# Gating a Pool load queue on VectorE, with a new order of all steps: attention and an ELU layer on one Trainium2 core

## The chip, the cores and the metric

The kernel runs on one NeuronCore of a Trainium2 chip (trn2). The metric is the device time of one execution in microseconds (us); less is better. The engines work side by side, each through its own instructions in program order: TensorE (PE for its matmuls, PEld for its weight loads), VectorE (DVE), ScalarE (ACT), GpSimd (POOL) and SyncE (SP). Here POOL does little but issue loads and SP little but issue stores and transposing copies.

## The reference, cut to what matters

Attention with 16 extra keys ("beacons") ahead of 576 tokens, for 8 batches and 8 heads of width 64; then two matrix products with an ELU between them on all 4,608 tokens.

```python
scores = scale * np.matmul(q, k_all.transpose(0, 1, 3, 2))   # k_all: 16 beacon keys, then k
scores = np.where(causal, -1000000000.0, scores)
a = np.exp(scores - scores.max(-1, keepdims=True))
a /= a.sum(-1, keepdims=True) + 1e-09
attn_out = np.matmul(a, v_all)
# ... (cut: heads side by side, x is 4608 x 512)
h = x @ w_in                                                  # 512 x 2048
g = np.where(h > 0.0, h, np.exp(np.minimum(h, 0.0)) - 1.0)
out = g @ w_out                                               # 2048 x 512
```

All inputs and the output are float32. The kernel computes in 16 bits and accumulates in float32.

## The kernel before

The kernel is a list of 1,597 short words, each of which is one step. A loop reads the list from the front and emits the step's instructions. The framework orders engines by data: it adds the semaphores that the tiles' reads and writes require. So the list sets only the order of instructions on each engine, which step takes which buffer, and with that when an engine may start.

```python
    for word in """
    warm.11.128.bank.0 lq.0.0.0.2 lq.0.1.0.2 lq.0.1.4.8 lq.0.0.2.4 lq.0.1.2.4 id tri lq.0.0.4.8 bs
    # ... (cut: 1,597 words in all)
    s.9.3 os.8.3
    """.split():
        f, *args = word.split(".")
        op[f](*[int(a_) if a_.isdigit() else a_ for a_ in args])
```

The first number of a word is the batch b (or the token tile t: tiles 0 and 1 have 256 tokens, 2 to 9 have 512), and then come head pair p, chunk or block. What each kind of word does, and where:

| word | engine | step |
|---|---|---|
| lq, ld, lv, lb, wi, wo | POOL issues | loads that cast float32 to 16 bits: q and k of batches 0 and 1 (lq) into SBUF; q and k of later batches (ld, four parts each) into DRAM; v (lv, five parts) and beacon v (lb); w_in (wi, eight parts) and w_out (wo, four) |
| ct | SP issues | two transposing copies of q and k of one head pair, DRAM to SBUF |
| s, os | SP issues | store of an output tile |
| T, S, L/W, Y/Z | PE | transposes (batches 0 and 1), scores, sums and value products of batch 0, of later batches |
| F, G | PE | product with w_in; product with w_out, in four quarters |
| warm | PE | filler matmuls on zeros |
| x, n/N, e | ACT | exponential of scores; reciprocal of the sums as exp(-ln); exponential of the ELU |
| m, a, M/V, r, g | DVE | causal mask; partial sums; scaling by the reciprocal; min(e,1)-1; max(h, r) |
| cp, o | ACT (A) or DVE (V) | copies out of PSUM |
| cb | DVE | beacon keys into the key tile |

The loads, all on GpSimd's queue, and the transposing copies on SyncE's:

```python
    @step
    def lq(b, i, h0, h1):

        if (b, i) not in st:
            st[b, i] = attn.tile([PR, H, R, D], BF16, tag=f"et{next(slots['et'])}", bufs=1, name="stg")
        nc.gpsimd.dma_start(
            out=st[b, i][:, h0:h1, :, :].rearrange("p h r d -> p h (r d)"),
            in_=(q, k)[i][b, h0:h1, :, :].rearrange("h (p r) d -> p h (r d)", r=R),
        )
    # ... (cut)
    @step
    def ld(b, i, s0):

        if (b, i) not in st:
            st[b, i] = dram.tile([S, H, D], BF16, tag=f"qk{i}", name="qkd")
        s1 = s0 + S // 4
        nc.gpsimd.dma_start(
            out=st[b, i][s0:s1], in_=(q, k)[i][b, :, s0:s1].rearrange("h s d -> s h d"))

    # ... (cut)
    @step
    def lv(b, j):
        r0 = NB if j == 0 else 0
        n_ = kc[j] - r0
        nc.gpsimd.dma_start(
            out=v_tile(b)[r0:r0 + n_, j, :, :],
            in_=v[b, :, ilo[j]:ilo[j] + n_, :].rearrange("h s d -> s h d"))

    # ... (cut)
    def wi(part_, g_):

        f0, f1 = DF // 4 * part_, DF // 4 * (part_ + 1)
        nc.gpsimd.dma_start(out=w_in16[:, 2 * g_:2 * g_ + 2, f0:f1], in_=wi_v[:, g_, :, f0:f1])
    # ... (cut)
    @step
    def wo(i):
        nc.gpsimd.dma_start(out=w_out16[:, 4 * i:4 * (i + 1), :], in_=wo_v[:, 4 * i:4 * (i + 1), :])
```

```python
    @step
    def cb(b, p):
        nc.vector.tensor_copy(out=keys(b, p)[:, 1, 0:NB], in_=bkT[:, p, NB * b:NB * (b + 1)])

    @step
    def ct(b, p):

        for i in range(2):
            nc.sync.dma_start_transpose(
                out=keys(b, p)[:, i, NB:SK], in_=st[b, i][:, 2 * p:2 * p + 2, :].rearrange("s h d -> s (h d)"))

```

The scores of one chunk and the value products (with ones in place of v: the sums), as TensorE has them:

```python
    def score(b, p, s, c0, c1, o0):

        t = keys(b, p)
        for (j, qa, qe, col) in lays[b]:
            a, e = max(c0, col), min(c1, col + qe - qa)
            if a >= e:
                continue
            for h in range(2):
                nc.tensor.matmul(
                    out=s[:, h, o0 + a - c0:o0 + e - c0],
                    lhsT=t[D * h:D * (h + 1), 1, P * j:P * (j + 1)],
                    rhs=t[D * h:D * (h + 1), 0, NB + qa + a - col:NB + qa + e - col],
                    start=True, stop=True, skip_group_check=True,
                )

    # ... (cut)
    def quad(b, g, qa, qe, t, half, first):


        v16 = vt[b]
        pcs = [(j, max(a, qa), min(e, qe), c + max(a, qa) - a) for (j, a, e, c) in lays[b]
               if max(a, qa) < min(e, qe)]
        for n, (j, a, e, c) in enumerate(pcs):
            for i in range(4):
                h, p = 4 * g + i, 2 * g + i // 2
                nc.tensor.matmul(
                    out=t[32 * i:32 * (i + 1), a - qa:e - qa],
                    lhsT=ones[0:kc[j], :] if half is None else v16[0:kc[j], j, h, half::2],
                    rhs=ets[b, p][0:kc[j], i % 2, c:c + e - a],
                    start=(first and n == 0), stop=(n == len(pcs) - 1), skip_group_check=True)
```

The exponential of the scores, the logarithm and exponential that make the reciprocal (batch 0's step n.0.A), and the chain of the second half, where each F takes a PSUM bank until its g has read it:

```python
    @step
    def x(b, *k_):
        s, (p, c0, c1, o0) = et_part(b, *k_)
        if (b, p) not in ets:
            ets[b, p] = attn.tile([P, 2, ECOLS], FP16, tag=f"et{next(slots['et'])}", bufs=1, name="et")
        nc.scalar.activation(
            out=ets[b, p][:, :, c0:c1], in_=s[:, :, o0:o0 + c1 - c0],
            func=AFT.Exp, bias=0.0, scale=SCALE)

    # ... (cut)
    @step
    def n(b, g):
        src = lt[b, g]
        w = src.free_size()
        rl = rls[b, g] = attn.tile([P, 640], FP32, tag="rl", name="rl")
        dst = rl[:, 0:w]
        nc.scalar.activation(
            out=dst.rearrange("p (g c) -> p g c", g=2) if len(src.shape) == 3 else dst,
            in_=src, func=AFT.Ln, bias=0.0, scale=1.0)
        nc.scalar.activation(out=dst, in_=dst, func=AFT.Exp, bias=0.0, scale=-1.0)
    # ... (cut)
    @step
    def F(t, i):

        a, e = tiles[t]
        w = e - a
        h = hp[t, i] = bank(name="hps").rearrange("c (n w) -> c n w", w=w)
        k_ = a // TT
        for n_ in range(512 // w):
            fc = i * (512 // w) + n_
            for cc in range(NCC):
                nc.tensor.matmul(
                    out=h[:, n_, :], lhsT=w_in16[:, cc, P * fc:P * (fc + 1)],
                    rhs=xt[k_][:, cc, a - TT * k_:e - TT * k_], start=(cc == 0), stop=(cc == NCC - 1))
    # ... (cut)
    @step
    def e(t, i):
        eb[t, i] = melt.tile([P, 512], FP32, tag="e", name="e")
        nc.scalar.activation(out=eb[t, i], in_=flat(hp[t, i]), func=AFT.Exp, bias=0.0, scale=1.0)

    @step
    def r(t, i):
        rb[t, i] = melt.tile([P, 512], FP16, tag="r", name="r")
        nc.vector.tensor_scalar(
            out=rb[t, i], in0=eb[t, i], scalar1=1.0, scalar2=1.0, op0=ALU.min, op1=ALU.subtract)

    @step
    def g(t, i):
        w = tiles[t][1] - tiles[t][0]
        gt = gpool.tile([P, 512 // w, w], FP16, tag="g", name="gt")
        nc.vector.tensor_tensor(out=flat(gt), in0=flat(hp[t, i]), in1=rb[t, i], op=ALU.max)
    # ... (cut)
    @step
    def G(t, tb_, qd):
        if qd == 0:
            ob[t, tb_] = bank(name="ops")
        for fc in range(4 * qd, 4 * qd + 4):
            nc.tensor.matmul(
                out=ob[t, tb_], lhsT=gts[t, fc][:, P * tb_:P * (tb_ + 1)], rhs=w_out16[:, fc, :],
                start=(fc == 0), stop=(fc == NFC - 1))
    # ... (cut)
    @step
    def o(t, tb_, e_):
        osb = melt.tile([P, DM], FP32, tag="osb", bufs=5, name="osb")
        ENGINE[e_](out=osb, in_=ob[t, tb_])
        ob[t, tb_] = osb

    @step
    def s(t, tb_):
        row = tiles[t][0] + tb_ * P
        nc.sync.dma_start(out=out[row:row + P, :], in_=ob[t, tb_])
```

Which slot of a pool of buffers a step takes is read from digit strings, one for each pool ("et" for exponentials, "bank" for the four single PSUM banks, "qk" for the eight key tiles, "S" for the two double banks).

Of the kernel before, what the change touches and what calls it, by code (L numbers as in the profile page):

```python
# [17 lines left out]
def kernel(  # L18
# [11 lines left out]
    nc = tc.nc  # L30
    P = 128

    B, H, S, D = q.shape
# [23 lines left out]
            "085476123807654128370564128370564281"),  # L57
        "bank": (
            "03210320123012302100120312031230120201310312031203123211031023102312021032032123"
            "01231031021230210310321032101230201231023023021301201321032023012301231021001231"  # L60
            "231230123012302302310201302302310310"),
        "qk": (
            "07654132067541230657412630752413"),
        "S": (
            "01010101010101010101010101010101101010101010100110001101010101010010100101101011"
            "010101010100110101010010100101001011010101100101010101100101"),
# [512 lines left out]

    for word in """  # L580
    warm.11.128.bank.0 lq.0.0.0.2 lq.0.1.0.2 lq.0.1.4.8 lq.0.0.2.4 lq.0.1.2.4 id tri lq.0.0.4.8 bs
    T.0.0.1 T.0.0.0 lb.0 cp.0.0.1.A warm.4.64.bank.1 cp.0.0.0.V lq.1.1.0.4 S.0.0.2 lq.1.0.0.4 bt
    x.0.0.2 S.0.0.3 bk lv.0.1 T.0.3.1 x.0.0.3 T.0.2.1 cb.0.0 cb.0.1 S.0.0.1 cb.0.2 lv.0.2 cb.0.3
    T.0.1.0 cp.0.2.1.V x.0.0.1 S.0.0.0 T.0.1.1 cp.0.3.1.V wi.1.0 x.0.0.0 cp.0.1.1.V lv.0.0
    warm.2.64.bank.0 cp.0.1.0.A S.0.1.1 T.0.3.0 wi.1.1 x.0.1.1 S.0.1.0 cp.0.3.0.V T.0.2.0 lq.1.1.4.8
    x.0.1.0 warm.1.64.bank.2 cp.0.2.0.V S.0.3.0 x.0.3.0 S.0.3.3 m.0.0.0 wi.0.1 warm.2.64.bank.0
    cb.1.0 x.0.3.3 cb.1.1 m.0.1.0 S.0.2.0 warm.2.64.bank.0 x.0.2.0 S.0.1.2 warm.2.64.bank.0 wi.0.0
    x.0.1.2 S.0.2.3 m.0.2.0 warm.2.128.bank.0 lq.1.0.4.8 m.0.3.0 x.0.2.3 T.1.1.1 T.1.1.0 lv.0.3
    cp.1.1.1.A cp.1.1.0.V S.0.2.2 L.0.A x.0.2.2 S.0.2.1 lv.0.4 x.0.2.1 T.1.0.0 T.1.0.1 cp.1.0.0.V
    n.0.A wi.2.1 S.0.1.3 W.0.A.1 cp.1.0.1.V warm.1.64.bank.0 x.0.1.3 m.0.2.2 S.1.1 M.0.A.1 wi.2.0  # L590
# [12 lines left out]
    G.1.0.0 a.1.1.1 lv.2.2 x.1.7.2 r.1.4 F.1.7 a.1.0.2 g.1.4 lv.2.1 G.1.0.1 e.1.7 a.1.1.2 lb.2
    G.0.1.0 a.1.1.3 a.1.0.3 lv.2.3 a.1.0.4 r.1.7 Z.1.0.0 m.1.9.2 lv.2.0 Z.1.0.1 m.1.8.2 a.1.1.4
    cb.2.1 g.1.7 Y.1.0 ct.2.0 lv.2.4 m.1.11.3 G.1.1.0 N.1.0 m.1.12.3 cb.2.2 m.1.10.3 m.1.7.2 G.0.1.1
    a.1.3.1 a.1.3.2 G.1.1.1 V.1.0.0 ld.3.0.0 ct.2.1 G.0.1.2 V.1.0.1 a.1.2.1 G.0.0.2 V.1.0.2 a.1.2.2
    G.1.0.2 a.1.2.3 ld.3.0.144 ct.2.2 a.1.3.3 G.0.0.3 a.1.2.4 a.1.3.4 cb.2.3 ld.3.0.288 Y.1.1
    Z.1.1.1 ld.3.0.432 N.1.1 Z.1.1.0 ld.3.1.0 G.0.1.3 V.1.1.2 V.1.1.1 ld.3.1.144 G.1.0.3 o.0.1.A
    V.1.1.0 ld.3.1.288 cb.3.0 S.2.2 o.1.0.V S.2.1 x.2.2.0 F.2.5 cb.3.1 o.0.0.V s.1.0 ct.2.3
    ld.3.1.432 x.2.1.0 F.2.2 F.2.4 lb.3 m.2.1.0 e.2.2 e.2.5 r.2.2 S.2.0 S.2.3 g.2.2 x.2.0.0 G.1.1.2  # L610
    s.0.1 r.2.5 x.2.3.0 g.2.5 F.2.3 e.2.4 m.2.2.0 x.2.3.1 lv.3.0 F.2.0 r.2.4 m.2.3.0 e.2.3 g.2.4
    S.2.4 e.2.0 S.2.6 m.2.0.0 r.2.3 G.1.1.3 x.2.4.1 m.2.3.1 a.2.0.1 F.2.15 g.2.3 x.2.6.1 lv.3.1
    o.1.1.A a.2.0.2 F.2.6 e.2.15 r.2.0 m.2.4.1 x.2.6.2 lv.3.2 r.2.15 F.2.10 a.2.0.3 e.2.6 g.2.0
    lv.3.3 S.2.8 e.2.10 S.2.5 g.2.15 F.2.1 x.2.5.1 r.2.6 lv.3.4 r.2.10 F.2.7 g.2.6 e.2.1 cb.3.2
# [123 lines left out]
```

The softmax here doesn't subtract the row's maximum and nothing guards it: scores larger than these inputs give would overflow.

## Time and profile before

| what | value |
|---|---|
| median time of three runs | 350.19 us (349.31 to 350.23) |
| span of the profiled execution | 350.2 us |
| mean granted clock of TensorE | 0.994 |
| bytes moved by the casting loads | 18.49 MB of 35.82 MB |
| transposing copies | 48, median 7.2 us from issue to landing |
| q and k loads (ld) | 24 + 24, median 7.5 and 10.5 us to landing |

The page names groups by line of the program: line 176 is ld, line 193 lv, line 276 ct, line 295 S, line 332 x, line 523 F, line 533 e, line 538 r, line 545 g, line 554 G, line 567 the store. Busy time of TensorE includes filler matmuls and matmuls at a reduced clock, so a full digit in a slice is not the same as useful work at full rate. Times to landing run from the issue to the last byte.

### The profile page before, as it was taken

Reading aid. Unit: us, or ns where it says so; the run is one execution under the profiler, and the core shown is the slowest. Engines: PE = TensorE matmul, PEld = TensorE weight load, DVE = VectorE, ACT = ScalarE, POOL = GpSimd, SP = SyncE. Lnnn points to the kernel's source line nnn. Section 1 sums busy time; section 2 is a strip of 40 time slices with the busy share of each in tenths; the row PEclk is TensorE's granted clock in tenths of the full one; section 3 lists DMA queues with packets and bytes.
Section 4 is the critical chain, followed back from the end, with each engine's and each line's share of the span. In section 5 each row is a group of like instructions: output and inputs, shape, how many; then the busy total and the mean of one; then the engine's idle time right before and its main releaser. Section 6 shows DMA issues by size and latency. Waiting matters only on the chain.

```text
span 350.2 us, 8532 instructions
## 1 busy us (share of the span) xinstructions
PE 336.9 (96%) x3448; PEld 163.5 (47%) x3449; DVE 273.9 (78%) x737; ACT 215.9 (62%) x330; POOL 100.7 (29%) x126
## 2 busy tenths in 40 slices
PE   7889999999999999999997999999999999999995
PEld 3557664444444444444432444454444454444442
DVE  2757999699969995999687993998659979967711
ACT  2999871797467664967296565868299435544301
POOL 8757682747076005800490005000000000000000
PEclk9999999999999999999998999999999999999999
DMA  8999999999999966990399039950010004000203
GB/s 122 180 195 196 173 180 134 165 163 147 145 136 157 154 107 78 164 109 2 25 174 168 0 83 134 175 131 2 2 60 2 1 4 154 26 3 0 90 32 120
DMA packets 137944, 35.82 MB, mean 102 GB/s; under 512 B 126001, under 2 KB 133425, under 8 KB 137905
## 3 DMA queue, kind: packets, MB, share of 16 engines
q0 software_dynamic: 102240, 18.49, 69.2%
q1 hardware_dynamic: 34944, 16.52, 24.2%
q8 instruction: 27, 0.44, 0.5%
q10 hardware_dynamic: 720, 0.26, 0.3%
q14 instruction: 13, 0.10, 0.1%
HBM read 37.22 MB, written 16.52 MB: 153 GB/s over the span
## 4 chain that ended last, share of the span: by engine, by line
PE 71%; DVE 13%; DMA 5%; ACT 5%; SPq 2%; issue 2%; POOL 0%; POOLq 0%
PE ops L554 32%; PE hps L523 25%; PE sc L295 5%; DVE r L538 5%; DVE gt L545 5%; PE ut L361 4%; DMA qk<-qkd 4%; ACT et L332 3%; SPq L276 2%; PE lt L361 1%; ACT e L533 1%; DVE et L348 1%; DMA stg<-in_k_dram 1%; PE lt L465 1%; DVE ls L449 1%
## 5 line engine op out<-in xcount | busy, mean ns | idle before, releaser
L523 PE MATMUL hps<-xT,w_in 128*128 128x512 f16 (+1 forms) x640 | 139.7, 360 | 2.2 <-DVE gt L545 1.6
L554 PE MATMUL ops<-w_out,gt 128*128 128x512 f16 x576 | 137.6, 381 | 0.1
L332 ACT ACTIVATE et<-sc 128x1024 f16<-128x1024 f32 (+4 forms) x128 | 105.5, 867 | 17.2 <-PE sc L295 17.0
L533 ACT ACTIVATE e<-hps 128x512 f32<-128x512 f32 x144 | 84.8, 603 | 47.8 <-PE hps L523 44.1
L545 DVE TENSOR_TENSOR gt<-hps,r 128x512 f16<-128x512 f32 x144 | 97.4, 685 | 2.3
L523 PEld LDWEIGHTS <-w_in 128*128 128x128 f16 x640 | 59.9, 98 | 66.4 <-issue 11.7
L538 DVE TENSOR_SCALAR r<-e 128x512 f16<-128x512 f32 x144 | 67.0, 473 | 23.3 <-ACT e L533 22.8
L554 PEld LDWEIGHTS <-gt 128*128 128x128 f16 x576 | 54.3, 98 | 65.3 <-issue 3.9
L348 DVE TENSOR_TENSOR et<-et,triu 128x256 f16<-128x256 f16 (+6 forms) x185 | 39.1, 252 | 5.1 <-ACT et L332 5.0
L295 PE MATMUL sc<-qk 64*128 64x80 bf16 (+20 forms) x528 | 35.0, 249 | 4.6 <-DMA qk<-qkd 2.6
L193 POOL DMA_DIRECT2D v<-in_v_dram x40 | 34.4, 867 | 3.4 <-DMA w_in<-in_moe_w_in_dram 1.0
L295 PEld LDWEIGHTS <-qk 64*128 64x128 bf16 x528 | 17.8, 94 | 30.2 <-issue 21.7
L494 ACT ACTIVATE rl<-lt 128x576 f32<-128x576 f32 x14 | 9.1, 651 | 35.3 <-PE lt L361 35.3
L186 POOL DMA_DIRECT2D v<-in_beacon_v_dram x8 | 4.4, 549 | 91.6 <-PE ut L361 66.5
L449 DVE TENSOR_TENSOR ls<-ls,et 128x672 f16<-128x672 f16 (+2 forms) x84 | 29.7, 369 | 1.2
L420 DVE TENSOR_TENSOR xT<-ut,rl 128x448 f16<-128x448 f32 (+6 forms) x56 | 20.2, 415 | 10.9 <-ACT rl L495 10.9
L176 POOL DMA_DIRECT2D qkd<-in_q_dram x24 | 22.7, 1019 | 14.1 <-DMA v<-in_v_dram 5.2
L176 POOL DMA_DIRECT2D qkd<-in_k_dram x24 | 24.6, 1363 | 1.9 <-DMA w_in<-in_moe_w_in_dram 1.2
L361 PEld LDWEIGHTS <-v 128*32 128x32 f16 (+1 forms) x1248 | 20.6, 96 | 9.5 <-issue 3.6
L561 ACT COPY osb<-ops 128x512 f32<-128x512 f32 x18 | 10.4, 586 | 21.4 <-PE ops L554 21.1
L561 DVE COPY osb<-ops 128x512 f32<-128x512 f32 x17 | 11.5, 684 | 12.2 <-DMA out_dram<-osb 7.9
L361 PE MATMUL ut<-et,v 128*32 128x512 f16 (+4 forms) x560 | 19.4, 278 | 0.0
(49 smaller groups left out, 124.3 us busy)
## 6 DMA issues: line engine op xcount, KB each, us to landing
out_dram<-osb SPq DMA_DIRECT2D x35, 256.0 KB, 3.0
qkd<-in_k_dram POOLq DMA_DIRECT2D x24, 144.0 KB, 10.5
qkd<-in_q_dram POOLq DMA_DIRECT2D x24, 144.0 KB, 7.5
v<-in_v_dram POOLq DMA_DIRECT2D x24, 128.0 KB, 7.8
w_in<-in_moe_w_in_dram POOLq DMA_DIRECT2D x8, 256.0 KB, 9.8
w_out<-in_moe_w_out_dram POOLq DMA_DIRECT2D x4, 512.0 KB, 9.7
v<-in_v_dram POOLq DMA_DIRECT2D x8, 112.0 KB, 7.3
stg<-in_k_dram POOLq DMA_DIRECT2D x3, 288.0 KB, 6.4
```

The lines of the kernel that those rows point to most:

```text
L176: nc.gpsimd.dma_start(out=st[b, i][s0:s1], in_=(q, k)[i][b, :, s0:s1].rearrange("h s d -> s h d"))
L193: nc.gpsimd.dma_start(out=v_tile(b)[r0:r0 + n_, j, :, :], in_=v[b, :, ilo[j]:ilo[j] + n_, :].rearrange("h s d -> s h d"))
L295: nc.tensor.matmul(out=s[:, h, o0 + a - c0:o0 + e - c0], lhsT=t[D * h:D * (h + 1), 1, P * j:P * (j + 1)], rhs=t[D * h:D * (h + 1), 0, NB + ...
L332: nc.scalar.activation(out=ets[b, p][:, :, c0:c1], in_=s[:, :, o0:o0 + c1 - c0], func=AFT.Exp, bias=0.0, scale=SCALE)
L348: nc.vector.tensor_tensor(out=o, in0=o, in1=triu[0:kc[j], :, t0:t0 + e - a], op=ALU.mult)
L361: nc.tensor.matmul(out=t[32 * i:32 * (i + 1), a - qa:e - qa], lhsT=ones[0:kc[j], :] if half is None else v16[0:kc[j], j, h, half::2], rhs= ...
L449: nc.vector.tensor_tensor(out=lsum[b, p][0:kc[j], :, qj - q1:], in0=in0, in1=e_[0:kc[j], :, cj:cj + S - qj], op=ALU.add)
L523: nc.tensor.matmul(out=h[:, n_, :], lhsT=w_in16[:, cc, P * fc:P * (fc + 1)], rhs=xt[k_][:, cc, a - TT * k_:e - TT * k_], start=(cc == 0), ...
L533: nc.scalar.activation(out=eb[t, i], in_=flat(hp[t, i]), func=AFT.Exp, bias=0.0, scale=1.0)
L538: nc.vector.tensor_scalar(out=rb[t, i], in0=eb[t, i], scalar1=1.0, scalar2=1.0, op0=ALU.min, op1=ALU.subtract)
L545: nc.vector.tensor_tensor(out=flat(gt), in0=flat(hp[t, i]), in1=rb[t, i], op=ALU.max)
L554: nc.tensor.matmul(out=ob[t, tb_], lhsT=gts[t, fc][:, P * tb_:P * (tb_ + 1)], rhs=w_out16[:, fc, :], start=(fc == 0), stop=(fc == NFC - 1))
```

## The change

The change does three things. A word may carry a gate, written after a colon: the loop then adds a dependency of the load's instruction on the last instruction of the named step, which must stand earlier in the list. 110 of the 118 casting loads get one. The list is made anew, with these waits in the model that ordered it, and so are the digit strings of the slots. The purpose is to decide when a load may start, rather than to let each one go as soon as its buffer is free.

```diff
     slots = {
         "et": (
-            "085476123807654128370564128370564281"),
+            "087265413085671423058671423056817240"),
         "bank": (
-            "03210320123012302100120312031230120201310312031203123211031023102312021032032123"
-            "01231031021230210310321032101230201231023023021301201321032023012301231021001231"
-            "231230123012302302310201302302310310"),
+            "03210321032103213023212103210230321023012302010213023103201231231021320132021323"
+            "12310230230213231013201320312010321201320120123013031020301023103023102312001201"
+            "230132123102312310231301012032123013"),
         "qk": (
-            "07654132067541230657412630752413"),
+            "07165432061754230671543260175432"),
 ... (cut)
+    last = {}
     for word in """
```

The list (lines cut; the whole list is replaced):

```diff
-    warm.11.128.bank.0 lq.0.0.0.2 lq.0.1.0.2 lq.0.1.4.8 lq.0.0.2.4 lq.0.1.2.4 id tri lq.0.0.4.8 bs
-    T.0.0.1 T.0.0.0 lb.0 cp.0.0.1.A warm.4.64.bank.1 cp.0.0.0.V lq.1.1.0.4 S.0.0.2 lq.1.0.0.4 bt
 ... (cut)
-    cp.1.1.1.A cp.1.1.0.V S.0.2.2 L.0.A x.0.2.2 S.0.2.1 lv.0.4 x.0.2.1 T.1.0.0 T.1.0.1 cp.1.0.0.V
-    n.0.A wi.2.1 S.0.1.3 W.0.A.1 cp.1.0.1.V warm.1.64.bank.0 x.0.1.3 m.0.2.2 S.1.1 M.0.A.1 wi.2.0
 ... (cut)
-    lv.6.2 G.4.3.3 V.4.1.2 o.4.1.V lv.6.3 F.5.1 o.4.3.V s.4.1 lv.6.4 ct.6.1 F.5.2 e.5.1 r.5.1 S.5.2
-    e.5.2 cb.5.3 S.5.6 g.5.1 F.5.4 x.5.6.2 r.5.2 x.5.6.1 g.5.2 F.5.7 s.3.3 e.5.4 s.3.0 x.5.2.0 r.5.4
-    F.5.0 ct.5.3 g.5.4 e.5.7 S.5.3 o.4.0.V S.5.1 e.5.0 F.5.10 r.5.7 x.5.1.0 g.5.7 F.5.3 e.5.10 r.5.0
 ... (cut)
-    S.5.10 ld.7.0.288 r.5.6 x.5.5.1 F.5.12 cb.6.0 m.5.0.0 cb.6.1 g.5.6 ld.7.0.432 e.5.5 G.4.2.1
 ... (cut)
-    F.6.3 ct.6.3 x.6.0.0 r.6.0 lv.7.4 G.5.1.0 e.6.3 x.6.2.0 F.6.5 r.6.3 g.6.0 s.5.3 S.6.1 g.6.3
 ... (cut)
-    s.9.3 os.8.3
+    warm.11.128.bank.0 lq.0.1.0.2 lq.0.0.0.2 id lq.0.0.4.8 tri lq.0.1.4.8 bs T.0.0.0 T.0.0.1
+    cp.0.0.0.V warm.3.64.bank.1 lv.0.2:bs cp.0.0.1.A S.0.0.3 lq.0.1.2.4 bt x.0.0.3 S.0.0.2
+    lq.0.0.2.4 bk T.0.2.0 x.0.0.2 cb.0.0 wi.1.0 cb.0.1 S.0.0.1 cp.0.2.0.V T.0.3.0 S.0.0.0 cp.0.3.0.A
 ... (cut)
+    m.0.2.3 warm.2.64.bank.0 cb.0.3 cp.0.1.1.V x.0.2.0 lb.0:cb.0.3 S.0.3.2 T.0.1.0 wi.1.1:m.0.0.2
 ... (cut)
+    wi.2.1:cb.0.2 S.0.1.3 warm.1.128.bank.0 n.0.A m.0.3.3 W.0.A.0 lv.0.4 S.0.1.2 W.0.A.1 x.0.1.2
+    M.0.A.0 warm.2.64.bank.0 M.0.A.1 x.0.1.3 S.0.2.1 m.0.0.3 F.0.2 x.0.2.1 m.0.3.2 m.0.2.2
+    lv.0.3:m.0.3.2 T.1.0.1 e.0.2 T.1.0.0 wi.2.0:cp.0.0.0.V S.0.1.1 cp.1.0.0.V F.0.3 x.0.1.1
 ... (cut)
+    F.1.4 cb.2.2 g.1.0 x.1.9.2 a.1.0.4 a.1.1.3 G.0.1.0 ld.2.1.288:m.0.0.3 r.1.5 o.0.0.A a.1.1.4
 ... (cut)
+    Z.1.0.0 a.1.2.1 G.0.1.1 ld.2.1.144:o.0.0.A V.1.0.1 F.1.6 a.1.2.2 ld.2.0.288:a.1.1.1 a.1.3.2
 ... (cut)
+    a.2.0.2 r.2.10 lv.2.1:a.2.0.2 S.2.7 e.2.8 S.2.4 g.2.10 G.1.1.3 x.2.7.2 lv.2.0:a.1.2.1 g.2.15
 ... (cut)
+    x.2.10.3 ld.3.0.288:a.2.0.2 r.2.11 F.2.6 a.2.1.2 e.2.9 r.2.12 ld.3.0.432:a.1.2.4 a.2.1.3 Z.2.0.0
 ... (cut)
+    a.3.2.4 r.3.12 Y.3.1 g.3.12 Z.3.1.0 N.3.1 cb.5.1 cb.5.2 Z.3.1.1 cb.5.3 lv.4.1:cb.5.3 G.3.0.3
 ... (cut)
+    lv.5.3:m.4.0.0 V.4.0.0 G.4.0.1 s.3.3 e.4.12 s.3.0 g.4.8 lv.5.4:r.4.4 G.4.1.0 ct.5.1 V.4.0.1
+    F.4.15 r.4.12 m.4.7.2 g.4.12 G.4.0.2 e.4.15 a.4.3.2 r.4.15 G.4.3.0 ct.5.0 cb.6.1 a.4.2.1 G.4.1.1
+    a.4.2.2 a.4.2.3 G.4.3.1 g.4.15 a.4.3.3 G.4.1.2 ct.5.3 a.4.2.4 V.4.0.2 a.4.3.4 Y.4.1 Z.4.1.1
+    N.4.1 Z.4.1.0 G.4.1.3 V.4.1.2 V.4.1.1 G.4.3.2 V.4.1.0 S.5.1 o.4.1.V S.5.5 G.4.0.3 x.5.5.1 s.4.1
 ... (cut)
+    m.5.5.1 r.5.14 e.5.2 F.5.6 g.5.14 e.5.8 r.5.2 ld.6.0.0:g.5.14 S.5.0 e.5.6 S.5.2 g.5.2 F.5.11
 ... (cut)
+    a.5.2.3 a.5.3.1 F.5.15 V.5.0.2 a.5.3.2 G.5.0.1 a.5.3.3 e.5.15 ct.6.0 cb.7.1 a.5.2.4 V.5.0.1
+    G.5.3.2 a.5.3.4 V.5.0.0 Y.5.1 r.5.15 Z.5.1.0 r.5.13 N.5.1 g.5.13 Z.5.1.1 g.5.15 G.5.0.2 V.5.1.2
+    V.5.1.1 S.6.5 G.5.3.3 V.5.1.0 x.6.5.1 S.6.0 S.6.1 x.6.0.0 F.6.3 o.5.3.A F.6.14 e.6.3 s.5.3 S.6.2
+    ct.6.3 r.6.3 e.6.14 F.6.5 g.6.3 lv.6.2:r.6.3 x.6.1.0 G.5.0.3 lv.6.3:a.4.3.4 e.6.5 x.6.2.0 F.6.9
 ... (cut)
+    m.6.1.0 r.6.0 F.6.1 x.6.12.3 m.6.6.2 ld.7.1.0:r.6.0 r.6.2 m.6.3.0 G.5.1.3 g.6.0 x.6.9.3 x.6.9.2
+    ld.7.1.144:m.6.1.0 g.6.2 F.6.12 e.6.1 a.6.1.1 ld.7.1.288:g.5.15 G.5.2.0 o.5.1.V e.6.12 r.6.1
+    ld.7.1.432:m.6.3.0 F.6.13 a.6.1.2 g.6.1 G.5.2.1 lb.7:g.6.4 e.6.13 a.6.1.3 a.6.0.1 F.6.7 a.6.0.2
+    m.6.8.2 G.5.2.2 m.6.9.3 e.6.7 a.6.0.3 a.6.0.4 r.6.13 Z.6.0.1 a.6.1.4 r.6.12 Y.6.0 r.6.7 ct.7.1
+    g.6.12 Z.6.0.0 N.6.0 g.6.13 F.6.10 g.6.7 F.6.8 V.6.0.0 s.2.0 V.6.0.1 F.6.11 ct.7.0 e.6.8 V.6.0.2
 ... (cut)
+    S.7.3 x.6.10.3 G.6.3.2 ct.7.3 x.7.3.0 F.6.15 m.6.10.3 a.6.2.1 x.7.3.1 a.6.3.1 G.6.1.0 e.6.15
 ... (cut)
+    S.7.5 G.6.0.2 x.7.4.1 r.7.4 m.7.0.0 m.7.3.1 lv.7.0:m.7.0.0 F.7.10 g.7.4 x.7.5.1 m.7.4.1 g.7.12
 ... (cut)
+    G.9.3.0 G.9.1.2 G.9.2.1 G.9.3.1 G.9.2.2 G.9.1.3 G.9.0.1 o.9.1.V G.9.3.2 s.9.1 G.9.0.2 G.9.2.3
+    G.9.3.3 o.9.2.V G.9.0.3 s.9.2 o.9.3.V s.9.3 os.9.0
     """.split():
+        word, _, gate = word.partition(":")
         f, *args = word.split(".")
         op[f](*[int(a_) if a_.isdigit() else a_ for a_ in args])
+        last[word] = nc.cur_bb.bb.instructions[-1]
+        if gate:
+            tc.add_manual_dep(
+                last[word], last[gate].name,
+                mybir.DependencyInfo(mybir.DependencyClass.Sync, mybir.DependencyReason.DATA))
 # ---- launch: one core; inputs and outputs as the reference has them ----
 _INS = ['q', 'k', 'v', 'beacon_k', 'beacon_v', 'moe_w_in', 'moe_w_out']
 _OUTS = [((4608, 512), 'float32')]
```

## The prediction

> **What bounds the kernel now.** I read the page first (shares, slices), then busy time by stretch, the waits of TensorE, the chain that ended last, the waits of SyncE, and two timelines.
>
> ```profile
> PE 336.9 (96%) x3448; PEld 163.5 (47%) x3449; DVE 273.9 (78%) x737; ACT 215.9 (62%) x330; POOL 100.7 (29%) x126
> PE   7889999999999999999997999999999999999995
> ...
> PEclk9999999999999999999998999999999999999999
> DMA  8999999999999966990399039950010004000203
> ```
>
> TensorE is the bound and stays so: 96% busy, no other engine over 78%. Only three places are below 9 tenths: the first 27 us, the slice around 185 us, where the granted clock dips too, and the tail. The DMA engines are full for the first 120 us and mostly idle after 220 us.
>
> A floor from the list of steps: 144 F and 144 G of 4 x 512 columns at 0.86 us each in the chain (4 matmuls) are 248 us; scores, value products, sums, transposes and fillers fill most of the rest. So the order can only win what TensorE loses in gaps, half clock and pauses. The stretches say how much is in sight:
>
> ```profile
> 7.00:24.00 17.00, 14.93 (x305) 9.09 (x300) 11.14 (x34) 15.13 (x21) 12.03 (x17) 1.00 1.44 189
> 24.00:46.00 22.00, 21.16 (x333) 15.82 (x330) 18.74 (x54) 19.93 (x32) 16.06 (x19) 1.00 1.83 181
> ...
> 180.00:220.00 40.00, 37.05 (x362) 16.21 (x360) 30.31 (x87) 25.01 (x37) 8.23 (x10) 0.96 0.96 106
> 220.00:290.00 70.00, 70.00 (x739) 32.86 (x738) 58.95 (x165) 45.84 (x72) 0.00 (x0) 1.00 0.28 45
> ```
>
> Columns: length, busy PE, PEld, DVE, ACT, POOL, clock, DMA, GB/s. From 7 to 46 us TensorE idles 2.07 + 0.84 = 2.9 us while ScalarE is at 35.06 of 39 us: the exponentials of batch 0 set the pace. From 180 to 220 us it idles 2.95 us, and the clock of 0.96 costs 40 x 0.04 = 1.6 us more. From 220 to 290 us it idles not at all.
>
> The second place is one wait and what it caused:
>
> ```profile
> PE sc L295 <- DMA qk<-qkd: 2.6, 2, 1.9
> PE hps L523 <- DVE gt L545: 1.6, 4, 0.7
> ...
> SPq L567 <- DVE osb L561: 102.1, 7, 31.4
> ...
> 145.89 28.80 SPq L567 DMA_DIRECT2D out_dram<-osb  x2
> 174.93 2.61 SPq L276 DMA_TRANSPOSE qk<-qkd  x2
> 177.63 1.02 SPq L567 DMA_DIRECT2D out_dram<-osb  x2
> ...
> 180.14 8.69 DMA qk<-qkd
> ```
>
> SyncE runs stores and transposes in program order. Store s.4.1 stands there for 28.8 us until its output tile is evicted; behind it stand the transposes ct.6.1 and ct.5.3. So ct.5.3, whose inputs landed long before, is issued at 178.70 and 180.14, and its second half takes 8.69 us because the loads of batches 6 and 7 started at 171 us. S.5.10 waits 1.95 us. The other wait (0.62 us at 215.8) is S.6.0 for ct.6.0, again late in SyncE's queue. Transposes issued at 126 to 132 us, with no load in flight, landed in a median of 2.8 us; those at 178 to 184 us in 8.9.
>
> **What the Trainium skill says.** (1) "TensorE: Matmul & The Clock Gate", section "What's actually happening": the clock halves after about one idle window of 3.4 us and activity restores it. The trace agrees in part: a wait of only 1.95 us is enough, and after 189.27 us the chain has 4 matmuls in 1.82 and 4 in 1.69 us where others take 0.86: 1.8 us by these, 1.6 by the clock; I use 1.7. (2) "SBUF — State Buffer", section "Who interferes with whom": tensor_scalar can enter a 2-port mode and then excludes GpSimd from the shared ports, whoever is first; descriptors of Pool loads are written through them. The trace agrees: r (line 538) takes 6.98/17 = 0.41 us from 240 to 290 us, where Pool is idle, and
>
> ```profile
> 98.00:110.00 12.00, 3.19 (x5) 1.00 1.50 133
> ...
> 171.00:184.00 13.00, 3.90 (x6) 1.00 1.51 135
> ```
>
> 0.64 and 0.65 us in two bursts of 14 loads, with single ones at 1.06. (3) "DMA: Bandwidth & Descriptors", section "Issuing engines are not separate DMA queues": queues of different engines share the same DMA engines. The 2.8 against 8.9 us agree.
>
> **The change part by part.** *Work.* Both lists have 1,597 steps with the same counts of every kind but the engine of a few copies, and the same 29 filler matmuls. Nothing is computed more or less.
>
> *Gates.* 110 of 118 loads get a wait on an earlier instruction (104 on VectorE, 6 on a ScalarE copy). Many point to instructions long past; since Pool issues in order, only the latest so far binds. The binding ones break up the bursts: the v loads of batch 2 go to a.2.0.2, batch 4's v loads to cb.5.3, batch 7's to m.7.0.0, and the q/k loads of batch 5, 6 and 7 move about one batch later than now. A wait on Pool is free, as Pool has 249 us of idle time; its price is a later landing.
>
> *Start.* ScalarE sets the pace, so I count what stands before the first logarithm n.0.A: 13 exponentials and 3 copies now, 12 and 2 after: 0.867 + 0.645 = 1.5 us earlier for the first F (now 24.08 us). Some is lost to w_in: wi.1.1 is gated on m.0.0.2 behind cb.0.3, at some 13 us, and w_in loads take a median of 9.8 us. I keep -1.2 us.
>
> *Transposes.* In the new order ct.5.1, ct.5.0 and ct.5.3 stand ahead of s.4.1, and no load of batch 6 starts before g.5.14. ct.6.0 comes ahead of the stores of tile 5. The two waits (2.6 us) and the half clock (1.7 us) go: -4.3 us. One new case of the kind is left: ct.6.3 behind s.5.3, with 7 F, 4 G and 5 S (10.5 us of TensorE) until S.6.12 needs it; two issues of 1.3 us and 6 to 7 us of flight fit, just.
>
> *VectorE in bursts.* F waits 1.6 us for g in four places, three of them inside or just after a burst of loads (41.8, 105.3, 181.7 us). Shorter bursts, and more room between F and the F that used its PSUM bank before (57 of 108 pairs now stand 2.0 to 3.0 us of matmul time apart, 33 of 113 after): -1.2 us, which counts three quarters.
>
> *New waits.* The gates leave loads just in time. Batch 7: the last q/k load is gated on m.6.3.0; from there to S.7.3 are 8 G, 6 F, 3 S and the value products of one group, 14.2 us of matmuls, some 15 us on the clock. Against it: issue of the last four loads 4.5 us, flight about 5 us with few others in flight, two pairs of transposes 5 us and 2 us to land: 16.5 us, 1.5 us too late. Batch 2: from o.0.0.A to S.2.0 are 12.6 us of matmuls, some 14 us; two issues 2, flight 6, one pair of transposes 2.5, landing 2 to 6: 12.5 to 16.5 us. Batch 2's v: from a.2.0.2 to Z.2.0.0 are 5.1 us; three issues and a flight of 3 to 5 us make 6 to 7. W.0.B needs lv.0.3, gated on m.0.3.2 only 6.1 us earlier. Four places, each perhaps 1 us late with a chance of one half: +1.9 us, as the clock can halve once.
>
> *Tail.* Still a matmul of the last tile, a copy split between two engines, two stores: 0.
>
> Sum: 350.2 - 1.2 - 4.3 - 1.2 + 1.9 = 345.4 us.
>
> **The rivals.** (a) *The gates are too tight.* For: k loads issued at 132 to 149 us, in a burst of 14, took 10.3 us to land; instructions on VectorE run behind the place that the list gives them, so a gate opens late. Against: later loads meet a nearly idle queue, where v loads issued at 98 to 103 us landed in medians of 3.3 to 5.6 us. If four waits of 2 us arise and the clock halves after two of them: 350.2 - 6.7 + 8 + 3.4 = 355 us. (b) *Only the reordering counts, the gates nothing*, since most point to the past and the DMA engines share bandwidth anyhow: then the transposes' wait goes (-4.3) and the rest cancels: 346 us. (c) *The model is good everywhere*: besides the above, the small pauses at the many changes between F, S and G shrink and no new wait arises: 350.2 - 1.2 - 4.3 - 1.6 - 2.5 = 340.6 us. (d) *The gain is off the path*: the start is DMA-bound and gets its 1.2 us back when S.2.0 waits; 348 us.
>
> **Range and chances.** The floor of what is visible (idle and half clock before the tail, about 11 us) makes 340 a good lower end; case (a) with half its size makes the upper. Range 340.5 to 351.5 us. Faster by over 2% means under 343.2 us: it needs (c), 0.24. Slower by over 2% is over 357.2 us: it needs (a) at more than its full size, 0.04. Within 2%: 0.72.
>
> **What would show it.** Right, if TensorE has no wait for qk<-qkd between 180 and 220 us and no slice at half clock there; if the first F starts near 22.6 us; if r's mean falls from 473 ns; if Pool idle time names VectorE as releaser. The new waits would appear as sc waiting for qk<-qkd near 65 and 234 us, or ut waiting for v near 80 us. Wrong, if these sum to over 3 us, if the clock dips at a new place, or if the first F is no earlier.

## The result and the profile after

The changed kernel takes 345.77 us (median of four runs, 345.26 to 347.71), beside 349.97 us for the kernel before (349.31 to 350.23) on the same chip: a ratio of 0.9893, 95% interval 0.985 to 0.9936. The prediction was 345.4 us in a range of 340.5 to 351.5. The profiled span is 343.6 us, at a mean clock of 0.998.

The same lines of the page of the changed kernel:

```profile
PE 334.0 (97%) x3449; PEld 162.2 (47%) x3449; DVE 271.3 (79%) x739; ACT 214.0 (62%) x328; POOL 99.8 (29%) x126
...
PE   7999999999999999999999999999999999999995
...
PEclk9999999999999999999999999999999999999999
DMA  8999999559959959998919939997009001300033
```

The 8s of TensorE at the start are 9s now, and the weak slice around 185 us is gone, its clock dip with it. The loads no longer go all at the front: the DMA engines have pauses from 60 us on, and the last loads go out at 258 us.

The four stretches of the prediction (columns: length; busy PE, PEld, DVE, ACT, POOL; clock; DMA; GB/s):

```profile
7.00:24.00 17.00, 16.05 (x295) 9.38 (x294) 11.66 (x41) 15.23 (x21) 12.40 (x19) 1.00 1.37 171
24.00:46.00 22.00, 21.13 (x340) 15.04 (x335) 19.21 (x55) 18.98 (x29) 9.75 (x13) 1.00 1.39 190
180.00:220.00 40.00, 39.03 (x403) 17.79 (x402) 35.89 (x102) 29.62 (x47) 16.98 (x20) 1.00 1.20 104
220.00:290.00 70.00, 70.00 (x709) 32.74 (x707) 59.27 (x157) 41.27 (x64) 7.34 (x9) 1.00 0.49 73
```

From 180 to 220 us TensorE is busy for 39.03 us at full clock. After 220 us loads still run (GpSimd 7.34 us busy, 0 before), and TensorE does not notice: 70 of 70 us.

TensorE's waits, apart from one of 1.3 us for the zeros of the fillers that both kernels have:

```profile
PE ops L554 <- DVE gt L545: 0.9, 2, 0.5
PE tqk L262 <- DMA stg<-in_q_dram: 0.6, 1, 0.6
PE tqk L262 <- DMA stg<-in_k_dram: 0.6, 1, 0.6
PE sc L295 <- issue: 0.5, 1, 0.5
PE sc L295 <- DVE xT L504: 0.5, 1, 0.5
PE hps L523 <- DVE gt L545: 0.5, 1, 0.5
```

No line has sc waiting for qk<-qkd, where the kernel before had 2.6 us. The 0.5 us under "issue" are scores at 25.4 us, by the list S.1.2. A small wait of the old kind is left at S.5.1, near 170 us: in this trace only its weight load waits for qk<-qkd (0.6 us), and in two other traces with the same binding gates TensorE itself does, for 0.49 us (experiment 4) and 0.54 us (experiment 5). F waits 0.5 us for g (1.6 before), but G now waits 0.9 us for it.

What the gates do shows in GpSimd's idle time and in the landings of what it issues (last column of the second fence: median us to landing):

```profile
POOL v L193 <- DVE et L348: 41.0, 3, 34.9
...
POOL qkd L176 <- DVE gt L545: 20.9, 1, 20.9
```

```profile
qkd<-in_k_dram POOLq DMA_DIRECT2D x24, 144.0 KB, 5.4
qkd<-in_q_dram POOLq DMA_DIRECT2D x24, 144.0 KB, 5.2
```

The same loads took 10.5 and 7.5 us before. The transposing copies land in a median of 3.4 us, 7.2 before.

**Where the time went.** Starts in two traces can't be subtracted: the first F now starts at 20.89 us instead of 24.01, but it also stands earlier in the list. I therefore take from a step's start the duration at full rate of all TensorE work that the list puts ahead of it; what is left is the time lost until then. Matmuls that run side by side, in pairs or fours, are counted once, and 512 columns at 0.213 us. Measured chains of four take 0.86 us, which is 0.215 each, so a part of every entry is only this difference; what counts is the difference between columns. It is my own arithmetic on the traces; the last columns are experiments told below (Y is the first step of the value products of a head group, the first number its batch).

| lost until, us | before | changed | changed, again | old order, ct early | new order, no gates |
|---|---|---|---|---|---|
| first F | 10.67 | 8.93 | 9.12 | 11.20 | 9.36 |
| Y.1.0 | 15.04 | 14.21 | 15.49 | 15.21 | 14.89 |
| Y.4.1 | 26.75 | 24.25 | 26.01 | 26.67 | 26.71 |
| Y.5.0 | 33.17 | 27.21 | 29.37 | 28.97 | 29.84 |
| last G | 41.15 | 34.55 | 36.70 | 36.29 | 37.47 |

Over half of the 6.6 us between the second and third column falls between Y.4.1 and Y.5.0: 6.42 us lost before, 2.96 after. That is where S.5.10 waited. The fourth column is a second trace of the changed kernel: it loses 2.15 us more, 1.28 of them by Y.1.0. So a difference of 1 us between two single traces says nothing at the start; means of several do.

### The profile page after: what moved, and what is told of

Its sections match the earlier page's. It is cut to its first block, busy times and chain, and to the rows that moved or that the text cites. A ratio compares the mean times of both kernels' runs of the same rounds, so it can differ in the third digit from the quotient of the medians.

```text
span 343.6 us, 8564 instructions
## 1 busy us (share of the span) xinstructions
PE 334.0 (97%) x3449; PEld 162.2 (47%) x3449; DVE 271.3 (79%) x739; ACT 214.0 (62%) x328; POOL 99.8 (29%) x126
## 4 chain that ended last, share of the span: by engine, by line
PE 74%; DVE 14%; ACT 4%; DMA 4%; issue 2%; POOL 1%; POOLq 0%
PE ops L554 34%; PE hps L523 27%; PE sc L295 5%; DVE gt L545 5%; PE ut L361 4%; DVE r L538 4%; DMA w_in<-in_moe_w_in_dram 3%; ACT et L332 2%; DMA stg<-in_k_dram 2%; DVE ls L449 2%; DVE et L348 2%; PE lt L361 1%; ACT e L533 1%; PE lt L465 1%; PE ub L361 1%
## 5 line engine op out<-in xcount | busy, mean ns | idle before, releaser
L523 PE MATMUL hps<-xT,w_in 128*128 128x512 f16 (+1 forms) x640 | 141.3, 358 | 0.8 <-DVE gt L545 0.5
L554 PE MATMUL ops<-w_out,gt 128*128 128x512 f16 x576 | 139.5, 380 | 0.9 <-DVE gt L545 0.9
L545 DVE TENSOR_TENSOR gt<-hps,r 128x512 f16<-128x512 f32 x144 | 96.4, 683 | 1.6
L538 DVE TENSOR_SCALAR r<-e 128x512 f16<-128x512 f32 x144 | 64.9, 459 | 26.5 <-ACT e L533 25.7
L193 POOL DMA_DIRECT2D v<-in_v_dram x40 | 37.1, 994 | 118.1 <-DVE et L348 41.0
L348 DVE TENSOR_TENSOR et<-et,triu 128x224 f16<-128x224 f16 (+6 forms) x185 | 39.1, 253 | 4.7 <-ACT et L332 4.6
L295 PE MATMUL sc<-qk 64*128 64x128 bf16 (+19 forms) x528 | 35.2, 249 | 1.4 <-issue 0.5
L561 DVE COPY osb<-ops 128x512 f32<-128x512 f32 x18 | 12.2, 685 | 13.4 <-PE ops L554 13.4
L449 DVE TENSOR_TENSOR ls<-et 128x928 f16<-128x928 f16 x28 | 17.3, 630 | 0.0
```

Of the source, the lines that this page charges most:

```text
L193: nc.gpsimd.dma_start(out=v_tile(b)[r0:r0 + n_, j, :, :], in_=v[b, :, ilo[j]:ilo[j] + n_, :].rearrange("h s d -> s h d"))
L295: nc.tensor.matmul(out=s[:, h, o0 + a - c0:o0 + e - c0], lhsT=t[D * h:D * (h + 1), 1, P * j:P * (j + 1)], rhs=t[D * h:D * (h + 1), 0, NB + ...
L348: nc.vector.tensor_tensor(out=o, in0=o, in1=triu[0:kc[j], :, t0:t0 + e - a], op=ALU.mult)
L449: nc.vector.tensor_tensor(out=lsum[b, p][0:kc[j], :, qj - q1:], in0=in0, in1=e_[0:kc[j], :, cj:cj + S - qj], op=ALU.add)
L523: nc.tensor.matmul(out=h[:, n_, :], lhsT=w_in16[:, cc, P * fc:P * (fc + 1)], rhs=xt[k_][:, cc, a - TT * k_:e - TT * k_], start=(cc == 0), ...
L538: nc.vector.tensor_scalar(out=rb[t, i], in0=eb[t, i], scalar1=1.0, scalar2=1.0, op0=ALU.min, op1=ALU.subtract)
```

## The experiments

My theory was that the gain is the transposes ct.5.3 and ct.6.0, which stood behind stores in SyncE's queue and landed slowly among loads, and that the rest of the change brings about a microsecond. Its rivals were that the gates do nothing (b), and that the whole new order with its gates is good in many small places (c). The first four experiments ran on one chip, beside a median of 350.34 us of the kernel before; the next four beside 351.1; the last three beside 350.63. Compare ratios across the groups. All kernels do the whole computation. Medians and ranges are over all executions, while ratios and intervals leave out the few (in experiments 5, 7, 10 and 11) that ran at a lower clock and some per cent longer.

**1. The new order without gates** (each word loses what stands behind its colon):

```diff
-    lv.2.1:a.2.0.2
+    lv.2.1
 ... (the same for all 110 gates)
```

> The new order and the new slots, without any gate: each load goes as soon as its buffers are free. Order theory (the gain is the place of the transposes in SyncE's queue and the earlier first F; the gates add little): 346 to 348 us, no wait of TensorE for a transpose over 1 us, r (line 538) back up to 470 ns or more. Gate theory (the loads held back are what keeps transposes and VectorE quick): 349 us or more, transposes at 6 us or more to landing, and TensorE waits for qk or for g again.

347.73 us (346.47 to 348.37), ratio 0.9911, interval 0.988 to 0.9943. Transposes land in a median of 6.3 us again. Its trace has two of its waits in TensorE's timeline (start, us, the group, in brackets the idle time ahead of it and its releaser):

```profile
72.00 0.51 PE L295 MATMUL sc<-qk 64*128 64x256 bf16 x8 [1.15 <-DMA qk<-qkd]
```

```profile
115.08 2.75 PE L523 MATMUL hps<-xT,w_in 128*128 128x512 f16 x12 [0.81 <-DVE gt L545]
```

Neither is in the changed kernel. The time lies in the order theory's range; the landing of the transposes and the two waits are what the gate theory expected. The gates do something: rival (b) falls, if only by some 2 us. The new slots were not tried apart from the new order.

**2. The old order with ct.5.3 and ct.6.0 moved ahead of stores** (every head pair keeps its key tile). Only ct.5.3 goes ahead of s.4.1; ct.6.0 goes next to ct.6.1, which stands behind s.4.1 but ahead of the later stores:

```diff
-    S.4.4 ct.5.2 e.4.2
+    S.4.4 ct.5.2 ct.5.3 e.4.2
-    lv.6.4 ct.6.1 F.5.2
+    lv.6.4 ct.6.1 ct.6.0 F.5.2
 ... (and the two words left out where they stood)
```

> The order before, with the two steps ct.5.3 and ct.6.0 moved ahead of store s.4.1 in SyncE's queue, all key tiles in their old slots, nothing else changed. Order theory: the wait of 1.95 us, the 3.4 us at half clock and the wait of 0.62 us go, 345.5 to 347 us. Gate theory: the transposes stay slow among the loads and TensorE waits elsewhere, 348.5 to 350 us.

347.09 us (346.49 to 347.55), ratio 0.9897, interval 0.9868 to 0.9926: -3.25 us of the 350.34, by two words in a list of 1,597, and 0.1 us above the order theory's range. SyncE's timeline (an inserted line moved the line numbers up by one):

```profile
143.22 5.40 SPq L277 DMA_TRANSPOSE qk<-qkd  x4
148.66 25.96 SPq L568 DMA_DIRECT2D out_dram<-osb  x2
174.84 5.24 SPq L277 DMA_TRANSPOSE qk<-qkd  x4
```

The store still blocks the queue for 25.96 us, but the four transposes of ct.5.2 and ct.5.3 pass ahead of it. TensorE has no wait for qk<-qkd. The median landing of the transposes stays at 7.3 us: issued early enough, slow copies cost nothing here.

**3. The old order with its loads held back**: 56 loads, from the first of batch 4 on, get a gate on the VectorE step that stands last ahead of them in the list, as in

```diff
-    ld.4.0.0
+    ld.4.0.0:g.2.1
```

> The order before, and every load from ld.4.0.0 on (56 of them) gated on the VectorE step that stands last before it in the list, so that GpSimd can't run ahead of the list. The late stores and transposes on SyncE stay as they are. Order theory: ct.5.3 is issued at some 178 us as before and lands sooner only as far as the loads of batch 7 are out of its way: 347 to 349.5 us. Gate theory: the burst at 171 to 183 us is gone, ct.5.3 lands in 2 to 3 us and S.5.10 no longer waits: 345 to 346.5 us.

347.14 us (346.42 to 350.7), ratio 0.9916, interval 0.9886 to 0.9946. ct.5.3 is issued at 177.88 us, as late as before, and lands in time all the same, for the loads of batch 7 no longer run beside it: its two copies take 5.7 and 4.6 us, where the second took 8.69 before. That is slower than the gate theory's 2 to 3 us, but S.5.10 no longer waits, as it expected; the time lies in the order theory's range. GpSimd's timeline:

```profile
184.08 3.86 POOL L176 DMA_DIRECT2D qkd<-in_q_dram  x4 [8.21 <-DVE r L538]
```

One wait of 0.57 us for qk<-qkd is left, at 210.39 us (ct.6.0).

**4. The changed kernel with the 29 gates that bind**, those whose step stands later in the list than that of every gate ahead:

```diff
     lv.2.1:a.2.0.2
-    lv.2.0:a.1.2.1
+    lv.2.0
 ... (81 of the 110 gates left out)
```

> The changed kernel with 29 of its 110 gates: those whose step stands later in the list than the step of every gate before it on GpSimd's queue. The other 81 point to steps that an earlier load has already waited for, by the list. Both theories: the same time as the changed kernel within 0.5 us, 345.3 to 346.3 us; a difference over 1 us would mean that a gate on another engine or an early step holds GpSimd after all.

345.79 us (344.78 to 346.63), ratio 0.9858, interval 0.9824 to 0.9893. No difference from the changed kernel shows, so the other 81 gates do nothing that these runs can tell.

**5. The changed kernel again**, nothing edited.

> The changed kernel once more, unchanged, beside the others of this set. Every theory: 345 to 346.5 us; it gives the distance between the changed kernel and its variants on one chip.

346.29 us (344.78 to 350.32), ratio 0.9861, interval 0.9823 to 0.9898.

**6. The old order with both cures** (the edits of 2 and 3 together).

> The order before with both cures at once: ct.5.3 and ct.6.0 ahead of store s.4.1, and the 56 loads from ld.4.0.0 on held to their place in the list. Theory that the two are substitutes (each alone removes the same wait at S.5.10 and the half clock after it): 346 to 347.2 us, at most 1 us better than either alone. Theory that they add up: 343.5 to 345 us.

347.27 us (346.73 to 349.62), ratio 0.9904, interval 0.9868 to 0.9939. Two cures worth 3.25 and 3.2 us alone are worth no more together: they cure the same wait.

**7. The changed kernel without the 26 gates ahead of batch 2's first load.**

```diff
-    lv.0.2:bs
+    lv.0.2
 ... (the same for 25 more, up to ld.2.1.432)
```

> The changed kernel without the 26 gates of the loads that stand ahead of ld.2.1.432, all later gates kept. If the gates earn their 1.9 us later on (VectorE undisturbed by bursts, transposes quick), the start goes alone as well: 345.3 to 346.5 us. If the start is where they count (the weights kept from crowding out the first q, k and v), some 0.7 us or more is lost: 346.5 us or more, with TensorE idle longer before 46 us.

348.07 us by the median, but the 14 runs lie in two groups: seven of 345.24 to 346.96 us, and seven of 349.18 to 351.48 us whose mean clock is 0.976 to 0.980 instead of 0.999 to 1.000; ratio 0.9899, interval 0.986 to 0.9939. The profiled run is of the lower group and loses 0.7 us for a beacon v. What these gates are worth is left open.

**8. The changed kernel with tight gates**: 70 loads, from the first of batch 3 on, wait for the VectorE step last ahead of them.

```diff
-    ld.3.0.0:m.1.5.1
+    ld.3.0.0:m.2.6.1
-    ld.3.0.144:m.0.0.2
+    ld.3.0.144:cb.3.3
 ... (the same for 68 more)
```

> The changed kernel with every load from ld.3.0.0 on (70) gated on the VectorE step that stands last before it in the list, instead of on its own gate, which breaks the remaining bursts up. If bursts are what is left of VectorE's lateness, TensorE's waits for g (0.5 + 0.9 us) fall and r's mean goes below 455 ns: 344.3 to 345.5 us. If the model's gates are as good as the list places: 345.3 to 346.3 us. If the loads now land too late: over 347 us with waits for qk or v.

347.67 us (346.31 to 349.5), ratio 0.9907, interval 0.9871 to 0.9943. Now the waits come up that I had feared of the changed kernel, two of them:

```profile
99.91 0.64 PE L295 MATMUL sc<-qk 64*128 64x48 bf16 x12 [2.09 <-DMA qk<-qkd]
```

```profile
207.67 0.61 PE L295 MATMUL sc<-qk 64*128 64x512 bf16 x6 [1.74 <-DMA qk<-qkd]
```

TensorE's waits for g fall to 0.9 us in all and r to a mean of 441 ns, which buys less than the 3.8 us that these two cost.

**9 and 10. The crossed test in the new order.** If place in the queue and held loads are two cures of one wait, the new order must do with either and suffer without both. ct.5.3 goes back behind s.4.1, once with all gates and once with none:

```diff
-    G.4.1.2 ct.5.3 a.4.2.4
+    G.4.1.2 a.4.2.4
-    x.5.5.1 s.4.1 F.5.1
+    x.5.5.1 s.4.1 ct.5.3 F.5.1
```

> The changed kernel with the transposes ct.5.3 moved back behind the store s.4.1 in SyncE's queue, and its waits on VectorE kept. If the loads held back are a cure by themselves (the two cures are substitutes), the store releases the queue near 172 us, no load is in flight until about 182 us, the transposes land within 1.6 to 3 us, TensorE waits at most 2 us for them, and the time is 346.3 to 348.5 us. If the place in the queue is what counts, TensorE waits 4 us or more and the time is above 349.5 us.

> The changed kernel with ct.5.3 behind the store s.4.1 and without any of the waits on VectorE: neither cure. If the held transposes among loads are the mechanism, TensorE waits 5 to 7 us for qk<-qkd between 170 and 190 us, perhaps with a stretch at half clock behind it, and the time is 351 to 355 us. If the new order has moved the need of these transposes so far that their place no longer matters, there is no such wait and the time is that of the new order without waits, 347 to 349 us.

With gates 347.97 us (346.77 to 350.55), ratio 0.9921, interval 0.9894 to 0.9947. Without gates 358.53 us (354.14 to 361.95), ratio 1.0241, interval 1.0189 to 1.0292. Both traces issue ct.5.3 within 0.1 us of each other (start 172.25 and 172.32 us in SyncE's timeline); first with gates, then without:

```profile
176.33 0.45 PE L295 MATMUL sc<-qk 64*128 64x128 bf16 x6 [1.67 <-DMA qk<-qkd]
```

```profile
181.03 0.72 PE L295 MATMUL sc<-qk 64*128 64x128 bf16 x6 [6.29 <-DMA qk<-qkd]
```

With gates, both copies land in the time and the wait in the size that were expected: GpSimd is silent from 162 to 184.63 us, and they take 2.8 and 3.3 us. Without gates, the wait was expected, but the time is above the 351 to 355 us; only the profiled execution lies within. There GpSimd's timeline has a dozen loads issued from 169.67 to 180 us, and the copies take 6.7 and 7.3 us:

```profile
169.67 0.53 POOL L186 DMA_DIRECT2D v<-in_beacon_v_dram  x1 [24.58 <-PE ut L361]
170.19 4.20 POOL L193 DMA_DIRECT2D v<-in_v_dram  x5
174.35 3.85 POOL L176 DMA_DIRECT2D qkd<-in_q_dram  x4
177.74 1.37 POOL L176 DMA_DIRECT2D qkd<-in_k_dram  x1
...
```

And the clock halves behind the long wait. Its busy time by stretch, the clock third from the end:

```profile
178.00:180.00 2.00, 0.00 (x0) 0.00 (x0) 0.00 (x0) 0.00 (x0) 1.82 (x3) 0.72 1.84 149
180.00:182.00 2.00, 0.97 (x7) 0.37 (x8) 0.00 (x0) 0.60 (x2) 1.27 (x3) 0.50 1.89 228
...
184.00:186.00 2.00, 2.00 (x6) 0.71 (x5) 0.43 (x1) 0.20 (x1) 0.00 (x0) 0.58 1.62 157
```

From 181.03 us on TensorE works at half clock until 185.69 us (0.58 of the last stretch is 1.68 us at half), which costs half of 4.65 us, 2.3 us, besides the 6.29. Of the four combinations:

| new order, ratio to before | gates | no gates |
|---|---|---|
| ct.5.3 ahead of s.4.1 | 0.9858 to 0.9893 (three measurements) | 0.9911 |
| ct.5.3 behind s.4.1 | 0.9921 | 1.0241 |

If the two losses added up, the kernel with neither cure would be at 0.9911 + 0.9921 - 0.9871 (the mean of the first cell), some 0.996. It is at 1.024: the mechanism stands. The profiled execution without both lost less than most: its time is the 354.14 us at a mean clock of 0.990, the others are 356.46 to 361.95, and the slowest three have 0.967 to 0.971. So more time at half clock is at least part of what those lost besides; where they lost it is not in a trace.

**11. The changed kernel with the causal mask's step behind the load of k of heads 4 to 7** on GpSimd's queue, for the first transposes' sake:

```diff
-    lq.0.0.4.8 tri lq.0.1.4.8 bs
+    lq.0.0.4.8 lq.0.1.4.8 tri bs
```

> The changed kernel with the mask's step moved behind the load of k of heads 4 to 7 of batch 0 on GpSimd's queue. If the first part of the kernel is held by these loads, the transposes of T.0.2.1 are waited for 0.5 us less, and the time is 345.2 to 346.3 us; if something else holds them, the time is that of the changed kernel, 345.7 to 346.5 us. The two ranges overlap: the trace is to tell them apart by TensorE's wait for stg.

346.74 us (344.98 to 353.2), ratio 0.9884, interval 0.9863 to 0.9905. It is not quicker. Its trace can't tell the two expectations apart: that execution took 350.51 us and ran at half clock from 11.35 to 25.00 us, so its wait of 1.7 us for stg is not comparable with the 1.2 us of the changed kernel. No version of these beats the changed kernel.

## Why the prediction was right, step by step

The time was right, and its largest step is shown. Of the four terms, one is about right, two were too large a gain and one too large a loss; that the errors cancelled is luck.

**Transposes, -4.3: right mechanism, somewhat large.** Experiment 2 measures both copies together at -3.25 us. In the traces, Y.4.1 to Y.5.0 loses 6.42 us before and 2.96 to 3.36 in four traces with both cures in the new order (the changed kernel and experiments 4, 5 and 7), and ct.6.0's wait of 0.62 us is gone besides. The part that was mis-sized is the half clock: I counted all 1.7 us of the profiled execution as the kernel's, but not every execution has it. Of the 72 executions of the kernel before that ran beside the experiments, 31 have a mean clock of 0.995 or less, and they took 1.5, 2.0 and 1.9 us longer in the mean than the others of their chip. So this part is worth some 0.8 us by my estimate (31 of 72 times 1.9), and with the waits of 2.6 us makes 3.4, close to the 3.25 measured. Experiments 9 and 10 show the mechanism in the new order. What I did not see is that the change cures it twice: I counted the transposes' place and "no load of batch 6 starts before g.5.14" in one breath, and either would have done.

**VectorE in bursts, -1.2: right size, other reason.** From Y.1.0 to Y.4.1 the four traces of the old order (before and experiments 2, 3, 6) lose 11.71, 11.45, 11.36 and 11.64 us, mean 11.54. The new order without gates loses 11.82 and 11.46 (experiments 1 and 10), mean 11.64: the order alone wins nothing there. With the change's gates (changed kernel, experiments 4, 5, 7, 9) it is 10.04, 10.32, 10.53, 10.00 and 10.23, mean 10.22. So the gates bring 1.3 to 1.4 us. But r hardly became quicker: the group's line is, first before and then after the change,

```profile
L538 DVE TENSOR_SCALAR r<-e 128x512 f16<-128x512 f32 x144 | 67.0, 473 | 23.3 <-ACT e L533 22.8
L538 DVE TENSOR_SCALAR r<-e 128x512 f16<-128x512 f32 x144 | 64.9, 459 | 26.5 <-ACT e L533 25.7
```

459 ns against 473, and the waits of F and G for g together are 1.4 us, beside F's 1.6 us before. Nor does r follow the gates: without any it takes 467 ns in experiment 1, 450 in experiment 10 and 462 in experiment 2, and experiment 8 has it at 441 ns and still loses. What the two traces of the new order without gates show in place of my reason is TensorE waiting for batch 2's transposes among loads, 1.15 us at 72 us in experiment 1 and 1.44 us in three waits from 65 to 71 us in experiment 10, where experiments 4 and 5 wait 0.17 and 0.23 us. That is the mechanism of the first term, and about the size of the gain. A wait for g near 114 us (0.81 and 0.48 us) is there besides; the two were not separated by a run.

**Start, -1.2: too large in what is kept.** The first F comes at 20.89 us, earlier than my 22.6. But less of TensorE's work stands ahead of it. In lost time until the first F, the new order has a mean of 9.24 us in eight traces (8.80 to 9.96, experiment 11 left out), the old one 11.03 in four (10.67 to 11.23): -1.8 us, more than I predicted. At Y.1.0 it is 14.59 against 15.16: 1.2 us are lost again on the way, and -0.6 us are kept. I predicted a start time of an instruction whose place in the list had moved; it should have been a lost time.

**New waits, +1.9: this step failed.** I gave four places an even chance of 1 us each. None of them waited in the changed kernel's trace; experiments 4 and 5 show 0.17 and 0.23 us at batch 2. The one new wait of some size, 0.49 and 0.54 us of S.5.1 in the same two traces, is at a place that I had not named. Together that is 0.7 to 0.8 us in place of 1.9. The tightest by my sum was batch 7, "1.5 us too late". The available time was as predicted: m.6.3.0 ended at 219.30 us and S.7.3 began at 234.43, which is 15.1 us. The need was not. GpSimd's timeline and TensorE's:

```profile
218.82 3.79 POOL L176 DMA_DIRECT2D qkd<-in_k_dram  x4 [4.81 <-DVE et L348]
```

```profile
230.63 3.63 PE L554 MATMUL ops<-w_out,gt 128*128 128x512 f16 x16
234.19 0.62 PE L295 MATMUL sc<-qk 64*128 64x448 bf16 x10
```

Only the last of the four loads has that gate; the other three had gone from 218.82 on, so that the last issue ended 3.3 us behind the gate, not 4.5. And one of the four transposes was issued ahead of the last load. ct.7.0 landed at 232.97 us, 13.7 us after the gate, 1.5 us before its need. Batch 2's v landed at 80.69 us, 0.2 us before Z.2.0.0 at 80.88; ct.2.0 at 63.93, 0.7 us before S.2.0; lv.0.3 at 28.43, 0.6 us before W.0.B.1.0. The gates are just in time in all four places. Experiment 8 shows how little is between: gates a few steps later bring two waits of 2 us. I had worked each place out to a microsecond or so and taken the uncertainty of my sum for a chance of the kernel.

**Sum.** -0.6, -3.25, -1.3 and +0.5 (S.5.1; batch 2's wait is within the -1.3) make -4.65 us, where the medians give -4.2 in the first measurement and -4.6 and -4.8 in experiments 4 and 5 (predicted: -4.8). The profiled executions differ by 6.6 us, as that of the kernel before has its half clock and is some 2 us above its median.

**The rivals.** (a), gates too tight, is what experiment 8 makes of the kernel, not the change. (b), the gates do nothing, falls with experiments 1 and 4. (c), good everywhere, fails by size: from Y.5.1 to the last G the changed kernel loses 6.8 us, the old order with ct early 6.5. (d), the start's gain given back, came true in part: 1.2 us are lost again, but before Y.1.0 and not at S.2.0, which did not wait. Its 348 us also leave out the gain on VectorE; with the other terms kept, giving the start back makes 346.6.

## What to carry to other kernels

A queue that runs in order holds everything behind a store until that store's tile is written (26 to 29 us here); put copies whose inputs are long there ahead of such stores, and only then ask how fast they land. Two cures of one wait don't add up: cross them, as either alone may do all the work and the pair still guards against the loss of both (10 us here). Compare the same step in two orders by the time lost until it, not by its start, and take means of several traces where a microsecond matters.

## What was not expected of the hardware

Whether a short wait halves TensorE's clock depends on where it falls. In the kernel before, 1.95 us of idling were followed by 3.41 us at half clock; in experiment 8, idle times of 2.09 and 1.74 us ahead of scores left it at full rate (1.00 in the stretches 98 to 104 and 204 to 212 us). The clock records of the traces tell why. Every stretch that begins and ends with a change of the clock is a whole number of 3.413 us long: 184.32, 3.41 and 157.01 us in the kernel before (54, 1 and 46 times), 174.08, 6.83 and 167.25 us in experiment 10 (51, 2 and 49). So the clock is decided on a grid, which begins at another time in each trace (4.16 to 7.22 us).

Along this grid I summed the work of the matmuls in each window, at full rate as for the table. The window with the wait in the kernel before (185.81 to 189.22 us) holds work for 0.31 of its length, the two of experiment 8 for 0.39 and 0.40. The 13 traces have 1,291 windows at full clock. The 16 with 0.38 or less, 13 of them at the end of the kernel, are all followed by half clock; the 1,275 with 0.39 or more are not. A wait of 2 us can thus be free or cost another 1.7 us or more, depending on how much work its window still holds. In experiment 10 TensorE was idle from about 174.7 us, and the clock fell at 178.87 us, when the first empty window ended.

The Trainium skill ("TensorE: Matmul & The Clock Gate", section "What's actually happening") has such a free-running window of about 3.4 us, with which the grid agrees. It lets the clock fall after a whole idle window; here a window with work for 0.31 of it was enough, and the measurement decides.

Also, 16 DMA engines that are shared between queues, as the skill has it ("DMA: Bandwidth & Descriptors", section "Issuing engines are not separate DMA queues"), showed as a latency: the same two transposing copies, issued at the same time, landed in 2.8 and 3.3 us with no load in flight and in 6.7 and 7.3 us beside a dozen loads.
